# Moving two lighter transfer slots of a grouped 1x1 convolution, and recutting its last stores

## Chip, cores, metric

One core of one Trainium2 chip. The metric is the device time of one execution in microseconds; the span in a profile is some 2 us shorter than the time of the same run (475.3 and 477.0 us for the profiled run of before).

## The reference

The convolution has k = 1, so it is a block-diagonal matrix product over 262,144 pixels of 192 channels, in four groups of 48.

```python
def setup_inputs():
    H = W = 512; G = 4; Cg = 48; C = 192; k = 1
    x: (1, 512, 512, 192) bfloat16      w: (1, 1, 4, 48, 48) bfloat16
def reference(x, w):
    xg = x.reshape(B, H, W, G, Cg)
    return einsum('bhwgc,gcd->bhwgd', xg, w[0, 0]).reshape(B, H, W, C)
```

Each byte of x is read once and each byte of the output written once: 100.7 MB each way.

## The kernel before

Pixels go to 128 SBUF rows; a "column" is one pixel of each row (128 x 384 bytes). Loads fill a ring of three slots of 80 columns, stores leave from an output ring of 292 columns. PE transposes four columns at a time (a "group"), DVE copies the transposed data to SBUF, PE multiplies, ACT casts the result into the output ring. The program is written around the DMA engines. Most slots are full: one transfer of 128 rows. Two slots are "partial": rows 16 to 19 are left out, and the rest goes in four transfers, two of them on the POOL queue.

```python
OGRID = (72, 144, 220, 292)
LATE_COLS = 100
LATE_PART = 44
LAST_PARTS = (32, 16, 12, 8)          # columns of the last stores
FULL = (("sync", 0, 128, 128, 0),)    # queue, first row, rows, outer, columns less
PARTIAL = (
    ("sync", 0, 16, 4, 0), ("sync", 32, 64, 16, 0),
    ("pool", 20, 12, 3, 0), ("pool", 96, 32, 8, 0),
)
UNEVEN = (("sync", 0, 16, 4, 18), PARTIAL[1], ("pool", 20, 12, 3, 8), PARTIAL[3])
FRONT = ((6, PARTIAL), (11, UNEVEN))  # full slots ahead of each partial one
...
def plan_fields(npix):
    parts, head = [], sum(HEAD)
    for slots, blocks in FRONT:
        parts += [(head + BIG * slots, FULL), (BIG, blocks)]
        head = 0
    cols = npix - sum((n - b[4]) * b[2] for n, blocks in parts for b in blocks)
    ...                                # the rest is full columns
```

POOL serves the partial slots one after the other, and in each one the load before the store:

```python
for nth, u in enumerate(mixed):                      # gpsimd
    part = [p for p in u.pieces if not p.full]
    for p in part:
        filler()
        gp.wait_ge(t_done, freed(p))                 # the ring slot is free
        for n, dram, sbuf in transfers(xf, ring, p, ("pool",)):
            gp.dma_start(sbuf, dram).then_inc(ld_sem[ld_key[p.i, n]], 16)
    for p in u.pieces:
        for n in range(len(p.blocks)):
            gp.wait_ge(ld_sem[ld_key[p.i, n]], 16)   # all four have landed
    gp.sem_inc(ld_sem[unit_keys[u][0]], 16)          # PE may go on
    filler()
    gp.wait_ge(go_sem, nth + 1)                      # ACT has filled the output
    ...                                              # the slot's POOL stores
```

ACT issues each store one group after its last column is cast, and waits for an older store to land before it writes over it:

```python
for g in range(NG):                                  # scalar
    act.wait_ge(mm_done, g + 1)
    while todo and stores[todo[0]].g1 <= g - 1:
        issue(todo.pop(0))
    if over[g] is not None:
        landed(over[g])
    act.copy(out_columns(g)..., o_ps[...])           # cast PSUM to bfloat16
act.wait_ge(fin, min(2, NG))
while todo:
    issue(todo.pop(0))                               # the last store
```

## Time and profile before

| | before |
|---|---|
| median of six runs | 477.7 us (475.7 to 478.6) |
| span of the profiled run | 475.3 us |
| moved | 201.5 MB, 424 GB/s over the span |
| share of the three data queues | 99.4% of 16 engines' span |
| PE / ACT / DVE busy | 90% / 82% / 52% |
| store issued last | 469.98 us, 5.3 us before the end |

A page gives, for 40 slices of the span, the busy tenth of each engine, and below it the share of the 16 DMA engines' time that each queue's packets fill. PE multiplies and transposes, DVE and ACT copy and cast, POOL and SP only issue transfers here; q1 carries SP's loads, q10 ACT's stores and q0 POOL's transfers. A line of a timeline gives start and duration in us, engine, line of the kernel and operation, and in brackets how long the engine stood before it and for whom. A line of waits gives who waited for whom: us in total, times, longest. The prediction shows the lines of the kernel before.

### The profile page before, as it was taken

What the parts mean: (1) busy time and instruction counts of PE and PEld (TensorE: products, weight loads), DVE (VectorE), ACT (ScalarE), POOL (GpSimd) and SP (SyncE); (2) the same over time, 40 slices, a digit from 0 to 9 for tenths busy, and PEclk for the clock granted to TensorE, in tenths of its full rate; (3) what the DMA queues carried; (4) which work ended last, traced back from release to release, by engine and by line L of the source; (5) the groups of instructions that cost most, each with busy time, mean ns of one, the idle gap of its engine ahead of it and who ended that gap; (6) DMA issues with size and microseconds to landing.
All of it is one profiled execution on the core that took longest, in us unless ns stands there. A gap on an engine that the chain in (4) does not pass through costs nothing.

```text
span 475.3 us, 13576 instructions
## 1 busy us (share of the span) xinstructions
PE 429.1 (90%) x6178; PEld 387.4 (82%) x6178; DVE 246.8 (52%) x258; ACT 388.7 (82%) x515; POOL 8.1 (2%) x20
## 2 busy tenths in 40 slices
PE   4999999998998999999987997997897896999993
PEld 4988898887887888888877986886787785988882
DVE  2555655554555555555654553554543553555551
ACT  2898998887997989888886895896795894999884
POOL 1000000000001000000000000000000000000000
PEclk9999999999999999999998998999998998999997
DMA  8999999999999999999999999999999999999997
GB/s 325 438 390 432 430 427 433 433 430 436 426 430 432 427 436 427 427 436 434 434 426 433 435 429 429 432 430 429 433 431 427 413 433 438 410 434 431 429 422 334
DMA packets 9456, 201.54 MB, mean 424 GB/s; under 512 B 1776, under 2 KB 1776, under 8 KB 2288
## 3 DMA queue, kind: packets, MB, share of 16 engines
q1 hardware_dynamic: 4152, 98.02, 48.5%
q10 hardware_dynamic: 4520, 98.00, 48.2%
q0 software_dynamic: 768, 5.34, 2.7%
q8 instruction: 7, 0.11, 0.1%
q14 instruction: 9, 0.07, 0.0%
HBM read 100.68 MB, written 100.66 MB: 424 GB/s over the span
## 4 chain that ended last, share of the span: by engine, by line
PE 55%; DMA 29%; ACT 9%; another core or an unknown queue 4%; issue 1%; ACTq 1%; SPq 0%
PE o_ps L371 32%; PE xT_ps L351 23%; DMA out_dram<-oring 20%; DMA ring<-in_x_dram 9%; ACT oring L450 9%; ACTq L431 1%; SPq L321 0%; SPq L314 0%; ACTq L424 0%; ACTq L433 0%
## 5 line engine op out<-in xcount | busy, mean ns | idle before, releaser
L450 ACT CAST oring<-o_ps 128x768 bf16<-128x768 f32 x514 | 387.4, 801 | 80.5 <-PE o_ps L371 48.9
L413 DVE COPY xT_sb<-xT_ps 128x1536 bf16<-128x1536 bf16 x257 | 246.2, 958 | 216.6 <-PE xT_ps L351 216.6
L371 PE MATMUL o_ps<-wt,xT_sb 128*128 128x144 bf16 (+1 forms) x3084 | 289.3, 236 | 31.8 <-ACT oring L450 26.7
L371 PEld LDWEIGHTS o_ps<-wt,xT_sb 128*128 128x128 bf16 x3084 | 212.0, 99 | 70.5 <-ACT oring L450 60.8
L351 PE MATMUL xT_ps<-ident,ring 128*128 128x128 bf16 x3084 | 220.6, 222 | 5.1 <-DMA ring<-in_x_dram 5.1
L351 PEld LDWEIGHTS xT_ps<-ident,ring 128*128 128x128 bf16 x3084 | 188.7, 99 | 7.9 <-issue 3.6
L298 POOL DMA_DIRECT2D ring<-in_x_dram x4 | 2.2, 560 | 241.9 <-PE xT_ps L351 241.9
L289 POOL DMA_DIRECT2D fill<-in_x_dram x4 | 2.4, 604 | 56.2 <-DMA ring<-in_x_dram 56.2
L308 POOL DMA_DIRECT2D out_dram<-oring x4 | 2.2, 556 | 63.9 <-ACTq L433 63.9
L333 PE MATMUL o_ps<-w_sb,esel 48*128 48x48 bf16 x10 | 0.6, 210 | 2.8 <-DMA w_sb<-in_w_dram 2.8
L333 PEld LDWEIGHTS o_ps<-w_sb,esel 48*128 48x128 bf16 x10 | 0.5, 112 | 2.7 <-issue 2.7
L406 DVE CAST wt<-o_ps 128x480 bf16<-128x480 f32 x1 | 0.7, 657 | 3.4 <-PE o_ps L333 3.4
L450 ACT ACT_TABLE_LOAD x1 | 1.3, 1283 | 0.8 <-PEq L470 0.8
L276 POOL TENSOR_SCALAR_AFFINE_SELECT esel<-esel 48x272 bf16<-48x272 bf16 x1 | 0.4, 404 | 0.0
L273 POOL MEMSET esel<- 48x272 bf16 x1 | 0.3, 318 | 0.3 <-POOLq L470 0.3
L280 POOL TENSOR_SCALAR_AFFINE_SELECT ident<-ident 128x128 bf16<-128x128 bf16 x1 | 0.3, 284 | 0.0
L274 POOL MEMSET ident<- 128x128 bf16 x1 | 0.2, 200 | 0.0
L470 POOL MEMSET const-float32-0.0<- 128x1 f32 x1 | 0.1, 99 | 0.3 <-issue 0.3
L470 POOL MEMSET const-bfloat16-1.0<- 128x1 bf16 x1 | 0.1, 102 | 0.0
L470 POOL MEMSET const-uint8-127<- 128x1 uint8 x1 | 0.1, 102 | 0.0
L470 POOL MEMSET const-float32-1.0<- 128x1 f32 x1 | 0.1, 99 | 0.0
## 6 DMA issues: line engine op xcount, KB each, us to landing
ring<-in_x_dram SPq DMA_DIRECT2D x22, 3840.0 KB, 30.3
out_dram<-oring ACTq DMA_DIRECT2D x15, 3456.0 KB, 37.9
out_dram<-oring ACTq DMA_DIRECT2D x6, 3648.0 KB, 41.8
out_dram<-oring ACTq DMA_DIRECT2D x3, 1920.0 KB, 39.8
out_dram<-oring ACTq DMA_DIRECT2D x1, 4032.0 KB, 52.2
ring<-in_x_dram SPq DMA_DIRECT2D x2, 1920.0 KB, 27.1
out_dram<-oring ACTq DMA_DIRECT2D x1, 3072.0 KB, 42.6
out_dram<-oring ACTq DMA_DIRECT2D x1, 2688.0 KB, 42.9
```

Of the source, the lines that this page charges most:

```text
L276: gp.affine_select(out=esel[:], in_=esel[:], pattern=[[-1, ECOLS]], compare_op=AluOpType.is_equal, fill=0.0, base=ESHIFT, channel_multipli ...
L289: gp.dma_start(dst, src).then_inc(fill_sem[k], 16)
L298: gp.dma_start(sbuf, dram).then_inc(ld_sem[ld_key[p.i, n]], 16)
L308: gp.dma_start(dram, sbuf).then_inc(st_sem[i][n], 16)
L333: last = pe.matmul(o_ps[:, NOB - 1, col:col + CG], lhsT=esel[:, s0:s0 + 128], rhs=w_sb[:, g, :], start=True, stop=True, skip_group_check=True)
L351: last = pe.transpose(xT_ps[:, g % NXP, j * 128:(j + 1) * 128], xg[:, j * 128:(j + 1) * 128], ident[:])
L371: last = pe.matmul(o_ps[:, v % NOB, c0_:c1_], lhsT=xs[:, j * 128:(j + 1) * 128], rhs=wt[:, WOFF[tc]:WOFF[tc] + (c1_ - c0_)], start=(tc == ...
L406: dve.tensor_copy(wt[:], o_ps[:, NOB - 1, 0:WCOLS]).then_inc(wc_sem, 1)
L413: dve.tensor_copy(xT_sb[pair % NXS][:, 0:n * 2 * UC].rearrange("p (g c) -> p g c", g=n), xT_ps[:, b0:b0 + n, 0:2 * UC]).then_inc(e_done[pa ...
L431: act.dma_start(dram, sbuf).then_inc(st_sem[i][n], 16)
L450: act.copy(out_columns(g).rearrange("p (u c) -> p u c", u=2), o_ps[:, v % NOB:v % NOB + 2, 0:UC]).then_inc(fa_done[g % (2 * NTOK)] if g < ...
L470: nc = _bacc.Bacc("TRN2", target_bir_lowering=False, num_devices=1)
```

## The change

It moves the two partial slots to earlier places, in hope of a better balance between the DMA engines while the program runs, and cuts the end into larger stores.

```diff
-LAST_PARTS = (32, 16, 12, 8)
+LAST_PARTS = (40, 20, 12, 12)
...
-FRONT = ((6, PARTIAL), (11, UNEVEN))
+FRONT = ((4, PARTIAL), (10, UNEVEN))
```

## The prediction

The recorded text is cut, at the marks, where no trace or run of this case shows what it says: which rows belong to which DMA engine by number, which engines are usually slow, the order in which an engine serves its queues, a ceiling of the rate, and when a transfer counts as complete. No term of its sum is cut: it came to -0.6 + 0.1 + 0.1 = -0.4 us on 477.8.

"Engine 4" is the text's name for the one slow engine; the trace gives no numbers. In the packet records of before, from 56 us on, 306 packets took 15 to 150 ns over the median of their size (the text has 20 to 70), and 285 of them, 16.4 us in sum, fit into one chain. That rows 16 to 19 are that engine's is read from the runs with one slot and with none, further down: 481 and 490 us, with one engine alone at the end. That an engine has four rows of such a transfer fits the records: the packets of the uneven slot's 12-row POOL transfers ran at most three at a time, and in the changed kernel those of its 16-row transfers at most four. At 95 us POOL's first packets come in three series, those of each 3.3 us apart, as much as one packet of each of the three queues takes (1,138 + 1,138 + 1,025 ns). The read-only burst of step 3 is shown at the start alone: from 27 to 30 us, ahead of the first store packet, 28 packets took 157 to 1,198 ns over the median. The three later bursts aren't read-only, as told under step 3 below. The "semaphore write" of step 4 is a packet of 4 bytes in the records, 9 ns in the median.

> **What bounds the kernel now.** I read the page's first lines, then the DMA view, then the waits, then the busy time by stretches, then the timeline of the last 15 us, and at the end the single DMA packet records in the trace.
>
> The page's head and slices:
>
> ```profile
> span 475.3 us, 13576 instructions
> PE 429.1 (90%) x6178; PEld 387.4 (82%) x6178; DVE 246.8 (52%) x258; ACT 388.7 (82%) x515; POOL 8.1 (2%) x20
> ...
> DMA  8999999999999999999999999999999999999997
> ...
> q1 hardware_dynamic: 4152, 98.02, 48.5%
> q10 hardware_dynamic: 4520, 98.00, 48.2%
> q0 software_dynamic: 768, 5.34, 2.7%
> ```
>
> No slice but the first and the last has a DMA digit under 9, and the three queues' packets fill 48.5 + 48.2 + 2.7 = 99.4% of 16 engines' span. PE at 90% is the next candidate. The stretches tell which of the two it is:
>
> ```profile
> core 0: us, PE busy (x) PEld busy (x) DVE busy (x) ACT busy (x) POOL busy (x), PEclk, DMA share, GB/s
> ...
> 220.00:260.00 40.00, 35.84 (x513) 32.10 (x511) 20.12 (x21) 32.29 (x43) 0.00 (x0) 0.97 1.01 433
> ...
> 440.00:450.00 10.00, 9.71 (x144) 8.64 (x142) 5.75 (x6) 8.89 (x13) 0.00 (x0) 1.00 1.01 434
> ...
> 470.00:475.30 5.30, 0.00 (x0) 0.00 (x0) 0.00 (x0) 0.00 (x0) 0.00 (x0) 0.50 0.59 241
> ```
>
> PE is busy 90% of 220 to 260 us and 97% of 440 to 450 us, while the DMA share is 1.01 in both: PE has slack that it gives back when it is let, and the DMA engines have none until 470 us. The waits show that the compute side is held by transfers and not the reverse:
>
> ```profile
> ACT oring L450 <- DMA out_dram<-oring: 23.3, 10, 4.6
> PE xT_ps L351 <- DMA ring<-in_x_dram: 5.1, 3, 1.9
> PEld xT_ps L351 <- DMA ring<-in_x_dram: 2.0, 1, 2.0
> ```
>
> ACT waits 23.3 us for room in the output ring, PE only 7.1 us for loads; neither leaves the DMA idle.
>
> From the packet records I take the budget of one engine. A packet of 30,720 bytes takes 1,138 ns in the median, one of 24,576 takes 912, so 0.0368 ns a byte plus some 8 ns. With the median of each size, all packets sum to 466.7 us on each of 16 engines. What packets took beyond the median is 72.4 us in all, 4.5 us an engine. The first data packet starts 3.1 us after the span's start. In the last 2.4 us some engines are done and others not, worth 1.2 us of idle an engine. 466.7 + 4.5 + 3.1 + 1.2 = 475.5, against the span of 475.3. So a program with the same bytes on each engine can shrink only in the 4.5, the 3.1 and the 1.2.
>
> [...] The trace names no engine[...]: nearly all of the persistently slow packets form one chain, its packets taking 20 to 70 ns more than the median; it loses 16.4 us from 56 us to the end, some 3.8%; and only one of the 176 POOL packets (rows 20 to 31 and 96 to 127) and none of the 32 shortened packets of rows 0 to 15 is slowed. [...]
>
> [...] load and store packets alternate on each chain (1,138 and 912 ns at 200 us). So a partial slot's packets, on whichever queue, share the same engine time.
>
> [...] The median packet is 27.0 GB/s, times 16 is 432, and stretches reach 434. [...]
>
> **The change part by part.**
>
> 1. Slot contents. Both slots stay as they were, a PARTIAL one and an UNEVEN one. Each spares engine 4 four rows of 80 columns of 384 bytes, 122,880 bytes in and as many out: 245,760 bytes at 0.037 ns are 9.1 us, twice 18.2 us, which is near the 16.4 us and more that it loses by being slow. [...] All of this is the same after: pixels, bytes on each engine and the order of the POOL transfers. Gain or loss: 0.
>
> 2. Place. Working the plan through, the full and partial columns run 560, 80, 880, 80, 456 before and 400, 80, 800, 80, 696 after; 1,896 full columns in both. Counting from 0 with the head as a slot, the partial slots are 7 and 19 before, 5 and 16 after. POOL issued its first partial load at 90.9 us and its last at 304.6 us. They wait for 50 and 170 transposed pairs, so a pair takes 213.7 / 120 = 1.78 us. After, they wait for 30 and 140 pairs: 90.9 - 36 = 55 us and 304.6 - 53 = 251 us.
>
> Engine 4's lag by 3.8% (an estimate, counted from the first packet at 3 us). Before: 0.038 * 88 = 3.3 us at the first slot, then -5.8; +8.1 to the second gives 2.3, then -6.8; +6.5 to the end gives -0.3. After: 2.0, then -7.1; +7.4 gives 0.3, then -8.8; +8.5 gives -0.3. The end is the same, as it must be. The peak of lag falls from 3.3 to 2.0 us and the deepest lead grows from 6.8 to 8.8 us. A load takes 28.9 us in the median from issue to landing and a store 37.6 us, so an engine 9 us ahead still has packets queued. It doesn't run dry, and so neither lag nor lead costs engine time by itself.
>
> 3. What the smaller lag can give. When a store lands late ACT waits, output runs dry, and for some microseconds all engines only read; then packets take some 500 ns more. Such bursts stand at 185 to 197 us (3.5 us of extra packet time), 368 to 384 us (8.2) and 417 to 430 us (7.0): 18.7 / 16 = 1.2 us an engine. If half go, 0.6 us. The burst at the start, near 40 us, stays.
>
> 4. Stores. The plan has 33 in place of 32. One more transfer is 8 packets of 8 ns fixed time and one semaphore write of 9 ns an engine: 0.07 us.
>
> 5. The tail. The last stores are 40, 20, 12, 12 columns for 32, 16, 12, 8 (ahead of the 32 stands another of 40).
>
> ```profile
> 462.57 0.34 ACTq L431 DMA_DIRECT2D out_dram<-oring  x1
> 466.21 0.34 ACTq L431 DMA_DIRECT2D out_dram<-oring  x1
> 468.77 0.34 ACTq L431 DMA_DIRECT2D out_dram<-oring  x1
> 469.98 0.35 ACTq L431 DMA_DIRECT2D out_dram<-oring  x1
> ```
>
> 432 GB/s are 8.8 columns of 49,152 bytes a microsecond. At 469.98 us, 475.3 - 1.2 - 470.0 = 4.1 us or 36 columns are still to go. Before, 28 of them were already queued, 3.2 us; after, 24 are, 2.7 us. The last store's first packet came 1.8 us after its issue, so the queue still covers it on average. The engines that end 2.4 us early have about 1.6 us queued in the new plan: they might idle 0.2 us, but they aren't the last. The earlier issues I place at the same pace: 30 to 33 columns are queued ahead of the stores of 40, 20 and 12, against 33, 33 and 26 ahead of those of 32, 16 and 12 now. Cost: 0 to 0.3 us.
>
> Sum: -0.6 + 0.1 + 0.1 = -0.4 us on 477.8. The three runs of before span 2.9 us, and the profiled run took 477.0, so I centre on 477.2.
>
> **The rivals.**
>
> A: the lag is what holds the kernel[...]. Then the wait of ACT for stores (23.3 us) would shrink with the lag. For it: those waits come from 180 us on, before the second slot. Against: the engines never idle in those waits. Even if all bursts and half of the uneven end went, 1.8 us: about 475.5 us.
>
> B: the lead grows too large, engine 4 has nothing to do for a while, and what it didn't use comes back as lag at the end: 224 us now follow the last slot in place of 171. If 3 us of it were lost, 480 us. Against: 29 us of queued loads.
>
> C: the tail underruns, a pause in compute (PE clock at 0.50 in short stretches, as in some 3.4 us records here) falling near the end, where 2.7 us are queued in place of 3.2. That would add some 1 us: 478.5.
>
> D: the first partial slot at 55 us collides with the settling of the start, where the program still fetches instructions and PE has no backlog of stores. PE would wait for it, and a further read-only burst such as that at 40 us (13 us of packet time, 0.8 us an engine) follows: 478.
>
> **Range and chances.** All the rivals lie between 475.5 and 480. The budget leaves no way to 468 without moving fewer bytes, and 487 would need nearly 10 us of idle on every engine. I predict 477.2 us, with 474.6 to 479.8 holding it 8 times in 10: the spread of 2.9 us between runs and the 1 to 2 us of the rivals. Faster by over 2%: 0.01. Within 2%: 0.97. Slower by over 2%: 0.02.
>
> **What would show it.** The page after should again have 9 in every DMA slice but the ends, 201.5 MB and queue shares summing to 99% or more (step 1). POOL's first partial load should be issued near 55 us and the last near 251 us (step 2). ACT's wait for stores should be 15 to 25 us: 15 or less with a shorter span speaks for A (step 3). The final stretch from 470 us should again have a DMA share near 0.6, and the last store issue should stand about 5 us before the end (step 5). It would be wrong if a slice in the middle shows a DMA digit of 8 or less, or if the packets' sum beyond the medians moves by more than 30 us.

## The result

The changed kernel took 478.04 us in the median of six runs (476.8 to 478.5), the kernel before 477.73 us. The ratio is 1.0006, with a 95% interval of 0.9982 to 1.0031: no difference that six runs can tell.

From the page of the changed kernel:

```profile
span 475.5 us, 13579 instructions
PE 427.4 (90%) x6178; PEld 385.9 (81%) x6178; DVE 246.8 (52%) x258; ACT 388.3 (82%) x515; POOL 8.1 (2%) x20
...
DMA  8999999999999999999999999999999999999997
...
q1 hardware_dynamic: 4152, 98.02, 48.4%
q10 hardware_dynamic: 4664, 98.00, 48.2%
q0 software_dynamic: 768, 5.34, 2.7%
```

The row of DMA digits is the same, character for character, and the shares sum to 99.3%. Only q10, the ACT queue of the stores, has more packets: 4,664 for 4,520. That is 144, or 16 engines times 8 data packets and one of 4 bytes (the records have 536 of 4 bytes on q10 for 520), so exactly one more store.

The POOL timeline, of two windows, shows the slots in their new places:

```profile
56.84 1.11 POOL L298 DMA_DIRECT2D ring<-in_x_dram  x2 [54.20 <-PE xT_ps L351]
...
251.45 1.10 POOL L298 DMA_DIRECT2D ring<-in_x_dram  x2 [136.59 <-PE xT_ps L351]
```

Busy time by stretches: stretch, its length, busy us of PE, PEld, DVE, ACT and POOL, granted PE clock, DMA share, GB/s.

```profile
450.00:460.00 10.00, 9.67 (x142) 8.48 (x139) 5.71 (x7) 8.72 (x12) 0.00 (x0) 1.00 1.02 437
...
465.00:470.00 5.00, 0.00 (x0) 0.00 (x0) 0.00 (x0) 0.00 (x0) 0.00 (x0) 0.58 0.98 416
470.00:475.50 5.50, 0.00 (x0) 0.00 (x0) 0.00 (x0) 0.00 (x0) 0.00 (x0) 0.50 0.50 208
```

And the last store, from the timeline:

```profile
463.57 0.34 ACTq L431 DMA_DIRECT2D out_dram<-oring  x1
```

This is the one thing that did change. Compute is over and the last store issued at 463.6 us, 6.4 us sooner than before, and nothing came of it: from 465 to 470 us no engine computes, and the DMA share is 0.98. The transfers had that much left to do either way. By the packet records 80 columns, 9.2 us at 432 GB/s, were still to be moved when the last store was issued; before the change it was 27 columns or 3.1 us. I hadn't expected it; it is the plainest sign that the DMA engines set the time.

The waits (total us, times, longest):

```profile
ACT oring L450 <- DMA out_dram<-oring: 20.7, 11, 4.9
PE xT_ps L351 <- DMA ring<-in_x_dram: 2.9, 2, 1.5
```

ACT waits 20.7 us for stores in place of 23.3. From the packet records: the sum of the median durations is 466.7 us an engine in both; what packets took beyond it is 67.0 us in all in place of 72.4, so 0.3 us less an engine, but 5.0 of these 5.4 us lie in the first 50 us, ahead of either kernel's first partial slot (from run to run it is 25.5 to 31.9 us there); idle time in the last 15 us is 1.7 us an engine in place of 1.3.

### The profile page after: what moved, and what is told of

Same layout as the page of the kernel before. It is cut to its first block, busy times and chain, and to the rows that moved or that the text cites. A ratio compares the mean times of both kernels' runs of the same rounds, so it can differ in the third digit from the quotient of the medians.

```text
span 475.5 us, 13579 instructions
## 1 busy us (share of the span) xinstructions
PE 427.4 (90%) x6178; PEld 385.9 (81%) x6178; DVE 246.8 (52%) x258; ACT 388.3 (82%) x515; POOL 8.1 (2%) x20
## 3 DMA queue, kind: packets, MB, share of 16 engines
q10 hardware_dynamic: 4664, 98.00, 48.2%
## 4 chain that ended last, share of the span: by engine, by line
PE 54%; DMA 31%; ACT 8%; another core or an unknown queue 2%; issue 1%; ACTq 1%; SPq 0%
PE o_ps L371 31%; DMA out_dram<-oring 30%; PE xT_ps L351 23%; ACT oring L450 8%; DMA ring<-in_x_dram 1%; ACTq L431 1%; SPq L321 0%; SPq L314 0%; ACTq L424 0%; ACTq L433 0%
## 5 line engine op out<-in xcount | busy, mean ns | idle before, releaser
L289 POOL DMA_DIRECT2D fill<-in_x_dram x4 | 2.4, 602 | 53.6 <-DMA ring<-in_x_dram 53.6
## 6 DMA issues: line engine op xcount, KB each, us to landing
ring<-in_x_dram SPq DMA_DIRECT2D x1, 2304.0 KB, 10.9
```

The source lines that it names most:

```text
L289: gp.dma_start(dst, src).then_inc(fill_sem[k], 16)
```

## The experiments

The table after the last one collects the idle time that the packet records of each show. The theory under test is the budget: the time is the bytes of the most loaded engine at its own rate, plus what the queues leave idle. Its rivals: A, the slow engine's lag holds the program; B, a lead of that engine is lost; and that the two parts of the change cancel each other.

### The two parts alone

The slots moved, the last parts as before:

```diff
 (the changed kernel)
-LAST_PARTS = (40, 20, 12, 12)
+LAST_PARTS = (32, 16, 12, 8)
```

> The slots moved, the last parts left at 32, 16, 12, 8. Budget theory (each DMA engine has the same bytes, so place doesn't matter): 476.5 to 479, ratio 0.997 to 1.003; the wrap of the output ring cuts the tail here into 16, 32, 16, 8, 4, 8. Rival 'the two parts of the change cancel each other': outside that, at least 0.5% off, in the opposite direction from the run with the last parts alone.

478.09 us beside 476.87 for before on this chip, ratio 1.0030 (1.0005 to 1.0055). At the edge of what was expected and only just clear of zero. Compute was over at 465.3 us, early as in the changed kernel.

The last parts new, the slots as before:

```diff
 (the changed kernel)
-FRONT = ((4, PARTIAL), (10, UNEVEN))
+FRONT = ((6, PARTIAL), (11, UNEVEN))
```

> The last parts 40, 20, 12, 12, the slots left behind 6 and 11 full ones. Budget theory: 476.5 to 479, ratio 0.997 to 1.003. Rival 'the two parts cancel': at least 0.5% off, opposite to the run with the slots alone.

479.16 us, ratio 1.0049 (1.0016 to 1.0081): outside the budget theory's 1.003. The page's DMA row, one of its stretches and the last store in the timeline:

```profile
DMA  8999999999999999999999999999999999999987
```

```profile
460.00:465.00 5.00, 4.94 (x74) 4.29 (x72) 2.90 (x4) 4.29 (x7) 0.00 (x0) 1.00 0.77 326
```

```profile
472.49 0.34 ACTq L431 DMA_DIRECT2D out_dram<-oring  x1
```

The digit before the last is an 8, and the stretch shows where: from 460 to 465 us the DMA share is 0.77. The store issued at 463.52 us, of 40 columns, was the first in 8.5 us, and only some 6 columns were then left ahead of it. Idle time in the last 15 us is 2.6 us an engine against 1.3, and in the packet records 13 of 16 engines end within 0.15 us of each other, where those of before end over 2.4 us; I read that as engines that have waited for the same last store. This is the underrun of the tail of the prediction's rival C, though without the pause of compute near the end that C supposed: PE is busy 99% of that stretch, at full clock. It is a few tenths of a per cent. The cause of the late end is in part the cut: the plan gives 24, 40, 8, 12, 12, 12 columns here, as the output ring wraps in the middle of the last parts.

So the two parts don't cancel in opposite directions: each alone was slightly longer. Both interact through where the ring wraps, which cuts the tail of the slots-alone run into 16, 32, 16, 8, 4, 8. That the wrap explains its 0.3% isn't shown: its idle time in the last 15 us (1.8 us) is that of the changed kernel.

### No partial slots

```diff
 (the changed kernel)
-FRONT = ((4, PARTIAL), (10, UNEVEN))
+FRONT = ()
```

> No partial slots at all, all 2048 columns in full slots. Budget theory: the slow engine gets its full sixteenth, 12.58 MB or 466 us at the median packet, plus 3.8% slowness, 18 us, plus 2 us of the start's slow packets and 3 us before the first packet: a span of 488 to 491, some 490 us, ratio 1.02 to 1.03, with the other 15 engines done some 10 to 18 us earlier. Rival 'the slow engine is covered by the queues, so the partial slots buy nothing': 477 to 480.

489.55 us, ratio 1.027 (1.0241 to 1.0299), span 487.3 us, just under the 488 to 491 of the budget. The page's DMA row, and the stretches:

```profile
DMA  8999999999999999999999999999999999999691
```

```profile
480.00:487.30 7.30, 0.00 (x0) 0.00 (x0) 0.00 (x0) 0.00 (x0) 0.00 (x0) 0.50 0.05 21
```

A share of 0.05 is less than one engine of 16 (0.06), at 21 GB/s. In the packet records exactly one engine works from 10 us before the end. So the slots are worth some 12 us, and what they buy is the end of that one engine.

### One partial slot

Three columns are left off the 64-row transfer, so that the pixel count divides.

```diff
 (the changed kernel)
-FRONT = ((4, PARTIAL), (10, UNEVEN))
+ONE = (PARTIAL[0], ("sync", 32, 64, 16, 3), PARTIAL[2], PARTIAL[3])
+FRONT = ((10, ONE),)
```

> One partial slot in place of two, behind 10 full ones. Budget theory: the slow engine carries 9.1 us more than with two, half of what the run with none adds over them: a span of 479 to 482, a time of 481 to 484, ratio 1.007 to 1.014, with one engine working alone for the last 3 to 5 us. Rival (a threshold: the queues cover a lag of up to some 10 us at the end too): 477 to 479.

481.16 us beside 476.25, ratio 1.0100 (1.0075 to 1.0126), span 479.1. In the packet records the last engine ends 3.5 us after the next to last. So there is no threshold at which the queues cover the surplus: two slots, one and none give 477, 481 and 490 us. The steps are unequal (5 and 8 us); I put this down to the slow engine no longer being alone at the end with two slots.

### The slots as late as they go

```diff
 (the changed kernel)
-FRONT = ((4, PARTIAL), (10, UNEVEN))
+FRONT = ((19, PARTIAL), (2, UNEVEN))
```

> The same two slots as late as they go: behind 19 full slots and 2 further ones. The slow engine's lag then grows to some 13 us before the first relief. Budget theory: the same time, 476.5 to 480, as a lag of 13 us is below the 29 us a load is in flight. Rival A (the lag holds the kernel[...]): 482 or more, with PE waiting more than 15 us for loads or ACT more than 40 us for stores before the first slot.

492.81 us, ratio 1.0326 (1.0295 to 1.0357). The expectation of the budget theory was plainly missed: this is longer than with no partial slot at all. A wait that no other run had so far, and the stretches:

```profile
PE xT_ps L351 <- POOLq L302: 16.4, 1, 16.4
```

```profile
420.00:440.00 20.00, 3.60 (x33) 3.34 (x32) 1.35 (x2) 2.21 (x4) 0.56 (x1) 0.62 0.86 370
440.00:460.00 20.00, 19.66 (x281) 17.97 (x279) 10.94 (x12) 16.61 (x22) 0.00 (x0) 0.95 0.51 216
460.00:480.00 20.00, 18.53 (x272) 16.70 (x273) 11.03 (x12) 17.36 (x24) 1.10 (x2) 1.00 0.74 311
```

L302 is POOL's word to PE that the second partial slot has landed. PE stood 16.4 us for it, from 420 us on; then it worked at 98% from 440 to 460 us, but the DMA engines, with the loads all in, had only what PE gave them: 0.51. Lag (A) or something else? The signs that the expectation named for A are missing: ahead of the first slot PE waited 9.1 us for loads and ACT 13.5 us for stores, not 15 and 40. The trace pointed at POOL: it had issued the second slot's load at 392.9 us, right behind the first slot's store at 391.2 us.

### The same, with POOL's order changed

```diff
 (the run above)
     filler()
+for nth, u in enumerate(mixed):       # stores only after both loads
+    part = [p for p in u.pieces if not p.full]
     gp.wait_ge(go_sem, nth + 1)
     ... stores
```

> As the run with both slots late, but POOL issues both slots' loads ahead of both slots' stores, so that the second slot's load no longer queues behind the first slot's store. New theory from the trace of that run (POOL issued the second load at 393.4 us, only after the first store's at 391.2 us, and PE then stood 16.4 us): the stall goes, 477 to 481, ratio 1.00 to 1.01. Rival A (the slow engine's lag of some 13 us is what cost the time): 486 or more.

489.92 us beside 477.92, ratio 1.0233 (1.0175 to 1.0292). My new theory, as I put it, was missed: the wait at L302 is gone, yet only a few microseconds came back. The waits show what stands in its place:

```profile
ACT oring L452 <- DMA out_dram<-oring: 26.4, 9, 7.3
```

```profile
440.00:460.00 20.00, 11.14 (x134) 10.56 (x135) 4.91 (x6) 9.18 (x13) 1.08 (x2) 0.74 0.63 266
460.00:480.00 20.00, 19.63 (x288) 17.49 (x287) 11.42 (x12) 17.72 (x25) 0.00 (x0) 1.00 0.77 326
```

The edit moved the wait and didn't remove it. With the loads ahead, the first slot's POOL store was issued at 415.6 us in place of 391.2; its output space came free later, ACT waited up to 7.3 us in one place, and PE with it. The experiment is therefore no verdict on A.

### Late, but with more room between the slots

```diff
+FRONT = ((16, PARTIAL), (4, UNEVEN))
```

> The order of POOL left alone, slots behind 16 full slots and 4 further ones: lag before the first relief some 10 us, and the first slot's store is due before the second slot's load. Theory of the POOL order: 477 to 480. Rival A (lag): two thirds of the loss of the late run, 485 or more.

477.44 us beside 477.92, ratio 0.9991 (0.9939 to 1.0043). By the estimate of 3.8% the slow engine is some 10 us behind before its first relief here, and it costs nothing. A falls for lags up to that size; the late run's own lag, some 12 us by the same estimate, no run has with the slots apart.

### Early, with room between

```diff
+FRONT = ((2, PARTIAL), (4, UNEVEN))
```

> The opposite: slots behind 2 full ones and 4 further ones, so that the slow engine is some 13 us ahead after the second slot and loses it over the remaining two thirds. Budget theory: 476.5 to 480, ratio 0.997 to 1.006. Rival B (a lead that large leaves the engine without queued packets, and the lost time comes back at the end): 482 to 488.

477.50 us, ratio 0.9995 (0.994 to 1.005). So a lead of some 14 us by the same estimate isn't lost either, where the program runs undisturbed.

### The gap of two in the middle

```diff
+FRONT = ((10, PARTIAL), (2, UNEVEN))
```

> The two slots with only 2 full ones between them, as in the late run, but in the middle: behind 10 full ones, with 10 more after them. Theory N (what costs in the late run is that a stall near the end can't be caught up, whatever makes it): 477 to 480, with a stall visible near the second slot that PE makes good later. Rival G (the gap of 2 itself costs the time): 485 or more.

480.31 us beside 476.25 (478.9 to 484.8), ratio 1.0106 (1.0059 to 1.0152): between the two expectations, so neither theory holds alone. The wait, and two of the stretches:

```profile
PE xT_ps L351 <- POOLq L302: 12.3, 1, 12.3
```

```profile
240.00:260.00 20.00, 9.35 (x133) 7.97 (x130) 5.75 (x6) 9.40 (x13) 0.00 (x0) 0.78 1.01 431
...
380.00:420.00 40.00, 39.29 (x583) 35.51 (x581) 23.28 (x25) 36.22 (x49) 0.00 (x0) 1.00 1.00 432
```

Here is the stall again, 12.3 us, and PE loses more than half of 240 to 260 us. But the DMA share in that stretch is 1.01: what was queued covered it, and PE made it good later at 98%. The POOL timeline shows where the stall comes from:

```profile
216.67 1.10 POOL L308 DMA_DIRECT2D out_dram<-oring  x2 [23.54 <-ACTq L433]
217.76 0.56 POOL L289 DMA_DIRECT2D fill<-in_x_dram  x1
218.35 1.11 POOL L298 DMA_DIRECT2D ring<-in_x_dram  x2
```

The store and the load of the next slot go out within 2 us on the same queue. In the packet records, the store's data packets start from 221.5 to 239.7 us and the load's from 247.9 to 258.3: one after the other. In the 7 us between them the small filler transfer of L289, issued between the two, came to its end (it landed at 247.7 us); what the store and the filler each cost was not tested apart. The larger of the two POOL loads took 44.1 us to land; in the same run the first slot's took 27.7.

What did the 1% come from, then? In the packet records one engine has nothing to do for some 2 us near 282 us and again near 300 us while the others are busy, and one engine works alone for the last 3.3 us. That looks like B, the relieved engine running out of queued packets and missing that time at the end. The slow packets, by which I know that engine, stop at 281 us and come again at 294 us, which fits; but the trace names no engine, so this is a reading and not shown.

### Far apart, the second slot as late as in the late run

```diff
+FRONT = ((8, PARTIAL), (13, UNEVEN))
```

> The slots far apart, behind 8 full ones and 13 further ones, so that the second stands where it stands in the late run and the last field has the same 136 columns. Theory N (nearness to the end): 483 to 491, the DMA share falling under 0.9 after 440 us. Rival G (the gap): 477 to 480.

477.29 us beside 476.25, ratio 1.0016 (0.9990 to 1.0041). Theory N, that nearness to the end alone costs the time, falls. Half of the stretch in which the late run had 0.51:

```profile
450.00:460.00 10.00, 9.79 (x144) 8.62 (x143) 5.75 (x6) 8.53 (x13) 0.00 (x0) 1.00 0.98 418
```

Together with the run before: slots close together make PE stall; the stall costs little in the middle, where the DMA queues outlast it, and 3% near the end, where they don't. Closeness alone cost 1.1%, lateness alone 0.2%. The POOL order is shown as the cause of the wait at L302, which went when the order was changed, not of the whole 3%.

### The missing pixels taken evenly

```diff
 (the changed kernel)
+LEVEL = (PARTIAL[0], ("sync", 32, 64, 16, 6), PARTIAL[2], PARTIAL[3])
-FRONT = ((4, PARTIAL), (10, UNEVEN))
+FRONT = ((4, PARTIAL), (10, LEVEL))
```

> The changed kernel with the second slot's missing 384 pixels taken evenly from the 64-row transfer (6 columns of each of its rows[...]) in place of 18 columns of rows 0 to 15 and 8 of rows 20 to 31. Budget theory: [...] the spread of the engines' ends (some 4 us in the trace of the changed kernel, 2.4 us in that of before) shrinks and the time falls by 0.3 to 0.7 us: ratio to before 0.996 to 1.001. Rival[...]: 0.5 to 1.5 us longer.

478.44 us beside 477.92, ratio 1.0011 (0.9972 to 1.0050). The time tells nothing, being the same within an interval wider than the effect. The spread of the engines' ends is 4.5 us against 4.1 in the changed kernel, so the step that I argued from the budget isn't borne out: taking the missing columns from rows 0 to 15 and 20 to 31 alone isn't what makes that spread. The 0.3 to 0.7 us were an estimate.

### Larger stores at the end

```diff
 (the changed kernel)
-LATE_PART = 44
-LAST_PARTS = (40, 20, 12, 12)
+LATE_PART = 72
+LAST_PARTS = (72, 12)
```

> The changed kernel with the last parts 40, 20, 12, 12 run together into 72 and 12. By the prediction's step 5 (last store issued 5 us before the end, 54 columns still to move when the 72 are issued) the queue runs dry for some 3 to 5 us: 480.5 to 483, ratio 1.006 to 1.011. If the store queue is as deep as the trace of the changed kernel shows it (last store issued 12 us before the end, some 105 columns or 12 us still to move), the big store still lies behind 2 us of work: 477 to 479, ratio 0.998 to 1.004.

476.91 us beside 476.25, ratio 1.0021 (0.9996 to 1.0047). By my own step 5 this should have cost 3 to 5 us. The last store in the timeline, of a span of 475.2 us:

```profile
462.86 0.34 ACTq L431 DMA_DIRECT2D out_dram<-oring  x1
```

The store of 72 columns was issued at 460.95 us, when by the packet records some 20 columns, 2.2 us, were still queued ahead of it: just enough for the queue not to run dry (the DMA share is 0.98 from 460 to 465 us). So the expectation from the changed kernel's trace held.

### The idle time of all runs

Mean idle time of one DMA engine in the last 50 us of the span, from the packet records of each profiled run:

| slots behind | last parts | idle us | median us | ratio to before |
|---|---|---|---|---|
| 6 and 11 (before) | 32, 16, 12, 8 | 1.2 | 477.7 | 1 |
| 4 and 10 (changed) | 40, 20, 12, 12 | 1.6 | 478.0 | 1.0006 |
| 4 and 10 | 32, 16, 12, 8 | 1.7 | 478.1 | 1.0030 |
| 6 and 11 | 40, 20, 12, 12 | 2.8 | 479.2 | 1.0049 |
| 4 and 10 | 72, 12 | 1.4 | 476.9 | 1.0021 |
| 4 and 10, level | 40, 20, 12, 12 | 1.8 | 478.4 | 1.0011 |
| 16 and 4 | 40, 20, 12, 12 | 1.8 | 477.4 | 0.9991 |
| 2 and 4 | 40, 20, 12, 12 | 1.8 | 477.5 | 0.9995 |
| 8 and 13 | 40, 20, 12, 12 | 2.4 | 477.3 | 1.0016 |
| 10 and 2 | 40, 20, 12, 12 | 4.1 | 480.3 | 1.0106 |
| 10 only | 40, 20, 12, 12 | 5.9 | 481.2 | 1.0100 |
| none | 40, 20, 12, 12 | 14.4 | 489.6 | 1.0270 |
| 19 and 2, POOL reordered | 40, 20, 12, 12 | 12.3 | 489.9 | 1.0233 |
| 19 and 2 | 40, 20, 12, 12 | 15.2 | 492.8 | 1.0326 |

The medians come from different chips and rounds, so compare the ratios. Packet records overlap by a little, so the figure for 50 us can fall short of that for 15 us by 0.1. The late run has about 3 us more idle time ahead of those 50 us. The ratio follows the idle column over most of its range. No version beats both kernels by more than the noise, and there was no room for one: with the same bytes on each engine, the budget leaves only the 1.2 us here, part of the slow packets' 4.5 and the start to save.

## Why the prediction was right

It forecast 477.2 us (474.6 to 479.8) and "within 2%" at 0.97; measured 478.04, ratio 1.0006. Point by point:

- **The bound and step 1 (same bytes on each engine).** Right, and shown from two sides: 6.4 us of earlier compute bought nothing, and putting bytes back on the slow engine moved the time by about what the budget says (481 and 490 us). One term is misread, not its size: the first data packet starts 2.3 us after the span's start, and the last ends 0.8 us before the span does; the budget has both as 3.1 us at the start. And PE's 7.1 us of waiting for loads count one wait twice, on PE and on PEld: it is 5.1 us.
- **Step 2 (place is free).** POOL issued at 56.8 and 252.0 us, with 55 and 251 forecast. That lag and lead don't count held for slots behind 16 and 4 full ones and behind 2 and 4. It isn't general, though: the budget theory built on it failed for slots 2 apart. The step didn't ask what POOL does with two slots that overlap; in the changed kernel they are 10 apart and the question doesn't arise.
- **Step 3 (the smaller lag gives 0.6 us).** Not borne out. The packets' sum beyond the medians fell by 5.4 us, but by only 0.5 us from 50 us on, where the kernels differ: 0.03 us an engine. The bursts were also misread. Their times were taken on the clock of the packet records, which starts 10.9 us ahead of the span: in the profile's time the three stand at 174 to 186, 357 to 373 and 406 to 419 us, and that of the start near 29 us. And only the one at the start is read-only: beside each of the 47 packets that took over 150 ns too long after 100 us, seven engines on average moved stores. After the change two of the three are gone, but from 339 to 379 us packets took 17.4 us too long. ACT's wait for stores fell by 2.6 us. That the lag changed any of this isn't shown.
- **Step 4 (one more store, 0.07 us).** The packet count (8 data packets and one of 4 bytes on each of 16 engines) is exact; the cost is below what can be measured.
- **Step 5 (the tail).** Wrong in its mechanism, without effect. I took the compute's end from the kernel before, and so had 24 columns, 2.7 us, queued ahead of the last store, when it was 68 columns or 7.8 us. (For the kernel before, the step has 28; the packet records show 19, as the last packet ends 0.8 us before the span.) The last store was issued 11.9 us before the end, not about 5. The cost of 0 to 0.3 us stands by luck of that. The run with 72 and 12 shows it: the step's arithmetic gives 3 to 5 us there, and the measured ratio is 1.0021. Why compute ends at 463 to 465 us with the slots at 4 and 10 (467.5 us in the level run), and at 470 to 472 us with them at 6 and 11, stays open; it is one trace for each run. The traces suggest, untested, that a long wait of ACT for a store late in the program decides it: of the runs under 480 us in span, the four with one of over 3.5 us after 390 us (before, the last parts alone, level, and 8 and 13) issue their last store at 467.5 to 472.5 us, the seven others at 462.9 to 466.1.
- **The rivals.** A: not for lags to 10 us. B: not in the changed kernel; perhaps in the run with slots 10 and 2. C: its underrun seen, but in the run with the last parts alone and without a pause in compute there. D: no trace of it, though the seven packets of q8, the instruction queue, do start at 18 to 71 us in the kernel before; what packets took too long from 50 to 70 us is 2.6 us in the kernel before and 2.7 us in the changed one.

The direction of -0.4 us can't be confirmed or denied: the interval spans -0.9 to +1.5 us.

## What to carry to other kernels

Here, with the DMA engines busy to 99% and the bytes per engine unchanged, moving work in time was free as long as the queues stayed filled, and an earlier end of compute was worth nothing. Check what such a move does to the spacing of transfers that share a queue. With the slots behind 10 and 2, POOL issued a store and a load within 2 us, and the load's packets began 8 us after the last of the store's had (247.9 and 239.7 us). A stall of 12 us in the middle of this program was covered by queued transfers, and one of 16 us near its end came with 16 us more in the time. And ask of each engine, not of the sum, how many bytes it has: one engine that is 3.8% slow cost 12 us here until it was given some 4% fewer bytes than the others (18.2 of 466.7 us).
